# B and C of chunks 1 to 5 turned by VectorE's 32x32 transposes instead of TensorE's

## The chip, the cores and the metric

The kernel runs on one core of one Trainium2 chip. The metric is the device time of one execution in microseconds (us), lower is better; the time of before is the median of 8 runs. A profile is one further execution, recorded instruction by instruction.

Engines are named as the profile names them: PE is TensorE's matmul, PEld its weight load, DVE is VectorE, ACT is ScalarE, POOL is GpSimd, and SP is SyncE, which issues all DMAs of this kernel.

## The reference

Two blocks stand one behind the other. The first is a state-space scan over chunks (batch 4, 8 heads, 768 tokens, head size 32, state size 16):

```python
log_a = np.log(np.clip(a, 1e-06, 1.0))
for c in range(nc):
    cum = np.cumsum(la, axis=-1)
    L = np.exp(cum[:, :, :, None] - cum[:, :, None, :]) * causal
    M = np.einsum('bhin,bhjn->bhij', Cc, Bc) * L
    y_intra = np.einsum('bhij,bhjd->bhid', M, xc)
    y_inter = np.einsum('bhin,bhnd->bhid', Cc, state) * np.exp(cum)[:, :, :, None]
    y[:, :, sl] = y_intra + y_inter
    Bx = np.einsum('bhjn,bhjd->bhjnd', Bc, xc) * np.exp(cum[:, :, -1:] - cum)[:, :, :, None, None]
    state = np.exp(np.sum(la, axis=-1))[:, :, None, None] * state + np.sum(Bx, axis=2)
```

The second is a feed-forward layer over its output, 3072 tokens of 256 numbers, with 2048 hidden units:

```python
h = x @ w_in
relu6 = np.clip(h + 3.0, 0.0, 6.0)
out = (h * relu6 / 6.0) @ w_out
```

x, a, B and C come as float32. The two weights come as float64, so each word pair has to be decoded to float32 on the core.

## The kernel before

The 768 tokens are cut into 6 chunks of 128, and a chunk holds all 4 batches and 8 heads. The order of the work on every engine is written out by hand: each engine runs its instructions in program order, and SP issues the DMAs in program order too, so a DMA whose buffer isn't free holds back those behind it.

The program has a start and six passes. Pass k runs the feed-forward layer on chunk k, and in its gaps the scan of chunk c = k + 1; for chunk `ahead` = k + 2 it loads the data and makes the decays.

- *Start, to about 24 us.* Loads, logarithms, decays of chunk 0 and half of chunk 1, the scan of chunk 0.
- *Pass 0.* 16 calls of `mlp_in` (L445, h = w_in times y), into which the decoding of the weights is woven: 8 raw pieces of 1 MB (4 of w_in, 4 of w_out), 3 buffers, and `decode` (L154) in five steps on ACT and DVE each. `load_w` (L103) issues the next piece in the fourth step. Then 16 blocks of `first_out` (L533, the product with w_out), in four rounds i of four batches b; round i needs decoded piece 4 + i. Between the blocks stand the turn, the scores and the mixing of chunk 1, and sums of weights (`in_weight_sums`, L464, two halves of four sums; `weight_sums`, L556, four sums), which passes 1 to 5 need.
- *Passes 1 to 5.* The layer by sums of quarter blocks: 8 steps s of `early`, `lead`, `last` and `middle` (7 half products a step, L490), and 14 `out_units` (L599). In `lead` an odd and an even bank are begun; ACT copies one half of the odd bank to the even one, DVE the other half to `up` (L504). In `middle` DVE adds `up` to the banks (L516, L517); `last` then writes on the half of the even bank that L517 has read.

The scan of a chunk has these steps. *Turn* (L335): B and C lie with the token on the partition and (head, state) in columns; PE turns them with an identity, four 128x128 transposes a call into one bank `t_ps`, for two batches, two calls a chunk. ACT copies B turned to `bT` (L347); C turned is written twice, each time with the heads of the other parity zeroed, as `cT` (L359 on DVE, or L356 on ACT), so that two heads share one product; and C turned times the exponentials of the cumulative decay `eto` gives `csT` (L365). *Scores* (L369): bT times cT into four banks `cb`, then L384 multiplies them into the decay matrices `L`. *Mix* (L387): csT with the state, L with x, and the new state. *Keep* (L423) copies y out. *Sum_y* (L480) forms the sums of y that the next pass needs.

`load_bc` (L81) loads a chunk's C and B with two DMAs, by token, in runs of 64 bytes. `load_eto` (L250) spreads each row of cumulative decay over the 16 partitions of its head, with 8 DMAs. `load_decay` (L244) spreads such rows over all partitions; GpSimd masks them (`conceal`), and ACT takes the exponentials (`decay`, L312). `ends` and `carry` prepare the state's update on GpSimd.

The turn of chunk 1 stands in pass 0, after the first block of round 2. The turn of chunk c in passes 1 to 4 stands at steps 3 and 5 of the same pass that uses it.

## Time and profile before

| what | us |
|---|---|
| median of 8 runs (369.97 to 371.53) | 370.18 |
| the profiled execution | 370.77 |
| its span, first to last instruction | 369.1 |
| PE busy in it | 362.4 |
| DVE busy | 229.1 |
| ACT busy | 190.4 |
| POOL busy | 134.3 |

What lies around the span (370.77 - 369.1 = 1.7 us) is no instruction's. Busy times overlap between engines. PE's busy time counts matmuls from start to a modelled end, so consecutive ones overlap, and a wait can hide under the end of the one before; spacing of starts tells more. In the rows quoted below, "x8" is the number of instructions in a row, and "[0.29 <-DVE csT L365]" is idle time of the engine before it and what ended it. Rows with SPq are DMA issues: the time is that of SP's issuing, not of the transfer. DMAs moved 29.21 MB in 86689 packets, 75456 of them under 512 bytes.

### The profile page before, as it was taken

To read this page: it belongs to the slowest core of one execution; us is meant where nothing else is said; L and a number is where in the kernel's file an instruction comes from. 1 tells how busy PE (TensorE), PEld (TensorE's weight loads), DVE (VectorE), ACT (ScalarE), POOL (GpSimd) and SP (SyncE) were. 2 spreads that over 40 slices of the span, in tenths; PEclk is the share of its full clock that TensorE was granted. 3 is DMA by queue.
4 is the path that set the end of the run, shared out by engine and by line. 5 is a ranking of instruction groups with operands and counts; after the bars stand their busy time and mean duration, and the time that the engine had idled before them with its cause. 6 is when DMAs were issued, how large, how long until landed. Compare 5 with 4: busy or idle time off the path is not lost.

```text
span 369.1 us, 7275 instructions
## 1 busy us (share of the span) xinstructions
PE 362.4 (98%) x2893; PEld 307.9 (83%) x2893; DVE 229.1 (62%) x448; ACT 190.4 (52%) x414; POOL 134.3 (36%) x134
## 2 busy tenths in 40 slices
PE   7999999999999999999999999999999999999996
PEld 3664468778888899888899888999888989888996
DVE  7679999894897542787452688343588442488111
ACT  5858778776673830674650575560466100366100
POOL 1200020531499412099512088600058800057800
PEclk9999999999999999999999999999999999999999
DMA  8957999702790036910027830000000000000000
GB/s 164 207 220 172 165 372 118 254 5 76 239 114 3 2 97 204 120 10 2 2 55 247 93 36 0 2 17 15 28 3 1 2 2 30 28 1 2 2 28 28
DMA packets 86689, 29.21 MB, mean 79 GB/s; under 512 B 75456, under 2 KB 81248, under 8 KB 86656
## 3 DMA queue, kind: packets, MB, share of 16 engines
q1 hardware_dynamic: 86656, 28.76, 37.7%
q8 instruction: 22, 0.36, 0.4%
q14 instruction: 11, 0.09, 0.1%
HBM read 25.53 MB, written 3.23 MB: 78 GB/s over the span
## 4 chain that ended last, share of the span: by engine, by line
PE 84%; DVE 9%; ACT 4%; issue 1%; DMA 1%; ACTq 0%
PE even L490 19%; PE ob L599 17%; PE oa L599 17%; PE odd L490 14%; PE cb L376 4%; PE y L409 3%; PE o L540 3%; DVE gT L529 2%; DVE wm L178 2%; PE y L400 2%; ACT we L175 2%; ACT L L312 1%; PE t_ps L343 1%; PE d L289 1%; PE d L292 1%
## 5 line engine op out<-in xcount | busy, mean ns | idle before, releaser
L585 POOL TENSOR_TENSOR s<-gT 128x512 f32<-128x512 f32 x20 | 26.4, 1321 | 104.4 <-DVE gT L529 104.4
L490 PE MATMUL even<-ts,w_sum 128*128 128x256 f32 x160 | 48.2, 383 | 0.0
L524 ACT ACTIVATE gT<-odd,half 128x512 f32<-128x512 f32 x40 | 27.5, 687 | 35.4 <-DVE odd L517 35.4
L503 ACT COPY even<-odd 128x512 f32<-128x512 f32 x40 | 23.0, 575 | 43.0 <-PE odd L490 42.0
L312 ACT ACTIVATE L<-L,cum_n 128x128 f32<-128x128 f32 x144 | 43.2, 391 | 2.1 <-POOL L L303 2.1
L490 PE MATMUL odd<-yT,w_in 128*128 128x256 f32 x160 | 41.1, 379 | 0.0
L384 DVE TENSOR_TENSOR L<-L,cb 128x512 f32<-128x512 f32 (+1 forms) x56 | 30.4, 606 | 17.2 <-PE cb L376 17.2
L599 PE MATMUL oa<-w_out,gT 128*128 128x128 f32 x320 | 39.3, 278 | 0.0
L599 PEld LDWEIGHTS oa<-w_out,gT 128*128 128x128 f32 x320 | 38.1, 192 | 1.4 <-issue 0.2
L303 POOL TENSOR_SCALAR_AFFINE_SELECT L<-L 128x1024 f32<-128x1024 f32 x18 | 20.0, 1124 | 49.3 <-DMA L<-cum_d 49.1
L599 PE MATMUL ob<-w_out,s 128*128 128x128 f32 x320 | 37.8, 276 | 0.0
L599 PEld LDWEIGHTS ob<-w_out,s 128*128 128x128 f32 x320 | 36.5, 192 | 1.3 <-issue 1.3
L490 PEld LDWEIGHTS even<-ts,w_sum 128*128 128x128 f32 x160 | 29.9, 190 | 5.3 <-ACT up L510 1.5
L529 DVE SCALAR_TENSOR_TENSOR gT<-gT,odd 128x512 f32<-128x512 f32 x40 | 27.5, 687 | 9.9 <-ACT gT L524 9.7
L490 PEld LDWEIGHTS odd<-yT,w_in 128*128 128x128 f32 x160 | 30.1, 190 | 3.9
L524 ACT ACTIVATE gT<-even,half 128x512 f32<-128x512 f32 x40 | 27.8, 695 | 4.4 <-PE even L490 4.4
L529 DVE SCALAR_TENSOR_TENSOR gT<-gT,even 128x512 f32<-128x512 f32 x40 | 27.2, 680 | 4.4 <-ACT gT L524 4.4
L599 PE MATMUL ob<-t,gT 128*128 128x128 f32 x240 | 29.7, 277 | 0.0
L599 PEld LDWEIGHTS ob<-t,gT 128*128 128x128 f32 x240 | 28.0, 192 | 1.3 <-issue 1.3
L540 PE MATMUL o<-w_out,gT 128*128 128x256 f32 x128 | 28.9, 381 | 0.0
L504 DVE COPY up<-odd 128x256 f32<-128x256 f32 x40 | 16.9, 423 | 18.2 <-ACT even L503 14.4
L448 PE MATMUL h<-yT,w_in 128*128 128x512 f32 x64 | 27.7, 594 | 0.0
(110 smaller groups left out, 633.7 us busy)
## 6 DMA issues: line engine op xcount, KB each, us to landing
L<-cum_d SPq DMA_DIRECT2D x18, 512.0 KB, 6.5
raw<-in_moe_w_in_dram SPq DMA_DIRECT2D x4, 1024.0 KB, 8.2
raw<-in_moe_w_out_dram SPq DMA_DIRECT2D x4, 1024.0 KB, 8.8
xt<-in_x_dram SPq DMA_DIRECT2D x6, 512.0 KB, 8.6
out_dram<-res SPq DMA_DIRECT2D x20, 128.0 KB, 1.7
bc<-in_C_dram SPq DMA_DIRECT2D x6, 256.0 KB, 5.2
bc<-in_B_dram SPq DMA_DIRECT2D x6, 256.0 KB, 7.6
eto<-cum_d SPq DMA_DIRECT2D x40, 32.0 KB, 5.3
```

The costliest lines, as they stand in the source:

```text
L303: nc.gpsimd.affine_select(out=L, in_=L, pattern=[[0, NH], [1, P]], compare_op=ALU.is_ge, fill=-1e5, base=0, channel_multiplier=-1)
L312: nc.scalar.activation(L[:, h], L[:, h], AF.Exp, bias=cum_n[:, c, g:g + 1])
L384: nc.vector.tensor_tensor(out=L[:, :, hs], in0=L[:, :, hs], in1=cbs[q][:, in_pair], op=ALU.mult)
L448: nc.tensor.matmul(out=h.rearrange("p r i -> p (r i)"), lhsT=w_in[:, j, f * P:(f + 1) * P], rhs=yTs[k][:, j].rearrange("p b i -> p (b i)") ...
L490: nc.tensor.matmul(out=bank[:, r], lhsT=lhsT, rhs=rhs, start=start, stop=True, skip_group_check=True)
L503: nc.scalar.copy(out=even, in_=odd[:, 1:2].to_broadcast([P, 2, 2 * P]))
L504: nc.vector.tensor_copy(out=up[:, 1], in_=odd[:, 0])
L524: nc.scalar.activation(gTs[k][:, f], h.rearrange("p r i -> p (r i)"), AF.Relu, bias=half, scale=1.0 / 6.0)
L529: nc.vector.scalar_tensor_tensor(out=g, in0=g, scalar=1.0, in1=h.rearrange("p r i -> p (r i)"), op0=ALU.min, op1=ALU.mult)
L540: nc.tensor.matmul(out=o[:, b % 2], lhsT=gTs[0][:, f, b * P:(b + 1) * P], rhs=w_out[:, f], start=(f == 0 and b % 2 == 0), stop=True, skip_ ...
L585: nc.gpsimd.tensor_tensor(out=o, in0=p_, in1=q_, op=op)
L599: nc.tensor.matmul(out=bank[:, slot], lhsT=lhs[:, j], rhs=rhs[:, j], start=(clear and j == 0), stop=True, skip_group_check=True)
```

## The change

Chunk 0 is turned as before, by PE. For chunks 1 to 5:

- The turn is DVE's. Its transpose turns each 32x32 block by itself. C and B are loaded a second time in a layout for that (`by_pair`): partition group q holds heads 2q and 2q + 1, so a block has 32 tokens by (2 heads, 16 states); 8 DMAs each for C and B, with runs of 256 bytes. B by token is loaded as well, for the state's update; C by token no longer. All `by_pair` tiles share two buffers.
- C turned is written to `csT`, B turned to `bT`, for all four batches at once. Two multiplications by the parity give `cT` from `csT`, and then `csT` is multiplied by `eto` in place. The three tiles have one buffer each, not two.
- `load_eto` goes by batch: 4 DMAs over all 128 partitions in place of 8 over 16.
- In pass 0 the loads of chunk 1 are spread: B and the pieces of C at f = 0, the pieces of B at f = 4 (the fifth raw piece of the weights is issued at f = 3), x at f = 5. The loads of chunk 2 move behind the rows of chunk 2's decays.
- Chunk 1 is turned right behind the last weight piece, at (i, b) = (0, 0), and the exponential of its `eto` stands ahead of the decays. GpSimd's `carry` and `ends` stay at (2, 0), without the turn.
- The sums of weights move: the first half of `in_weight_sums` from (1, 0) to (2, 2), the second from (2, 1) to (3, 1), the first two of `weight_sums` from (2, 2) to (3, 2), the third from (3, 0) to the store half of pass 1, beside the fourth.
- Chunk 2 is turned in three parts at steps 1, 3 and 5 of pass 1. Chunk `ahead` is turned in unit 9 of the store half of passes 1 to 3, so chunks 3 to 5 are turned one pass earlier than before.

```diff
@@ -76,21 +76,42 @@
     a_sb = pre[:G, 0:2].rearrange("g t i -> g (t i)")[:, :S]
     nc.sync.dma_start(out=a_sb, in_=a.rearrange("b h s -> (b h) s"))
 
-    loaded = {}
+    Bs, bcs, xts = {}, {}, {}
 
     def load_bc(c):
+
+
         sl = slice(c * P, (c + 1) * P)
-        bc = loads.tile([P, 2, NB * NH, N], FP32, name="bc")
-        for j, src in enumerate((C, B)):
-            nc.sync.dma_start(
-                out=bc[:, j], in_=src[:, :, sl, :].rearrange("b h s n -> s (b h) n"))
-        loaded[c] = bc
+
+        def by_token(src, **where):
+            t = loads.tile([P, NB * NH, N], FP32, **where)
+            nc.sync.dma_start(out=t, in_=src[:, :, sl, :].rearrange("b h s n -> s (b h) n"))
+            return t
+
+        def by_pair(src):
+            t = loads.tile([P, 2, NB, 4, N], FP32, name="by_pair", tag="bc")
+            for b in range(NB):
+                for h in range(2):
+                    nc.sync.dma_start(
+                        out=t[:, h, b].rearrange("s a n -> s (a n)"),
+                        in_=src[b, h:NH:2, sl, :].rearrange("h (s a) n -> h s (a n)", a=4))
+            return t
+
+        if c == 0:
+            bcs[c] = [by_token(C, name="C", tag="bc")]
+            Bs[c] = by_token(B, name="B")
+            bcs[c].append(Bs[c])
+        else:
+            Bs[c] = by_token(B, name="B")
+            bcs[c] = []
+            for src in (C, B):
+                bcs[c].append(by_pair(src))
+                yield
 
     def load_x(c):
         sl = slice(c * P, (c + 1) * P)
-        xt = loads.tile([P, NB * NH, D], FP32, name="xt")
-        nc.sync.dma_start(out=xt, in_=x[:, :, sl, :].rearrange("b h s d -> s (b h) d"))
-        loaded[c] = loaded[c], xt
+        xts[c] = loads.tile([P, NB * NH, D], FP32, name="xt")
+        nc.sync.dma_start(out=xts[c], in_=x[:, :, sl, :].rearrange("b h s d -> s (b h) d"))
 
     w_in = const.tile([P, NK, DF], FP32, name="w_in")
     w_sum = const.tile([P, NF // 2, P], FP32, name="w_sum")
...
@@ -249,10 +271,10 @@
 
     def load_eto(c):
         eto = att.tile([P, NB, P], FP32, name="eto")
-        for h in range(NH):
+        for b in range(NB):
             nc.sync.dma_start(
-                out=eto[h * N:(h + 1) * N],
-                in_=cum_d[c, h:NB * NH:NH].unsqueeze(0).to_broadcast([N, NB, P]))
+                out=eto[:, b],
+                in_=cum_d[c, b * NH:(b + 1) * NH].unsqueeze(1).to_broadcast([NH, N, P]))
         etos[c] = eto
 
     cum_n = const.tile([P, NC, G], FP32, name="cum_n")
...
@@ -332,43 +354,56 @@
                 out=tmps[c], in0=states[c - 1],
                 in1=etos[c][:, :, P - 1:P].to_broadcast([P, NB, 2 * D]), op=ALU.mult)
 
-    def turn(c, p):
-
-
-        bc, xt = loaded[c]
-        pool, tag = (ps, "f") if c < 2 else (ps_o, "o")
-        t_ps = pool.tile([P, 4, P], FP32, name="t_ps", tag=tag)
+    def turned(c):
+        if c not in bTs:
+            bTs[c] = [att.tile([P, 2, 2, P], FP32, name="bT", bufs=1),
+                      att.tile([P, 2, 2, 2, P], FP32, name="cT", bufs=1),
+                      att.tile([P, 2, 2, P], FP32, name="csT", bufs=1) if c else None]
+        return bTs[c]
+
+    def turn(p):
+
+
+        c = 0
+        bT, cT, csT = turned(c)
+        t_ps = ps.tile([P, 4, P], FP32, name="t_ps", tag="f")
         for k in range(4):
             j, b = k // 2, 2 * p + k % 2
             nc.tensor.transpose(
                 out=t_ps[:, k],
-                in_=bc[:, j, b * NH:(b + 1) * NH].rearrange("s h n -> s (h n)"), identity=ident)
-        bT = att.tile([P, 2, P], FP32, name="bT")
-        nc.scalar.copy(out=bT, in_=t_ps[:, 2:4])
-        if c == 1 and p == 0:
-            from_start(c)
-            carry(c)
-            for b in range(NB):
-                ends(c, b)
-        cT = att.tile([P, 2, 2, P], FP32, name="cT")
-        if c == 1 or (c, p) == (0, 1):
+                in_=bcs[c][j][:, b * NH:(b + 1) * NH].rearrange("s h n -> s (h n)"),
+                identity=ident)
+        nc.scalar.copy(out=bT[:, p], in_=t_ps[:, 2:4])
+        if p:
             for t in range(2):
                 nc.scalar.activation(
-                    cT[:, :, t], t_ps[:, 0:2], AF.Copy, scale=parity[:, t:t + 1])
+                    cT[:, p, :, t], t_ps[:, 0:2], AF.Copy, scale=parity[:, t:t + 1])
         else:
             nc.vector.tensor_tensor(
-                out=cT, in0=t_ps[:, 0:2].unsqueeze(2).to_broadcast([P, 2, 2, P]),
+                out=cT[:, p], in0=t_ps[:, 0:2].unsqueeze(2).to_broadcast([P, 2, 2, P]),
                 in1=parity.unsqueeze(1).unsqueeze(3).to_broadcast([P, 2, 2, P]), op=ALU.mult)
-        csT = None
-        if c:
-            csT = att.tile([P, 2, P], FP32, name="csT")
-            nc.vector.tensor_tensor(
-                out=csT, in0=t_ps[:, 0:2], in1=etos[c][:, 2 * p:2 * p + 2], op=ALU.mult)
-        bTs[c, p] = bT, cT, csT
+
+    def turn_by_pairs(c):
+
+
+        bT, cT, csT = turned(c)
+        for t, out_ in zip(bcs[c], (csT, bT)):
+            nc.vector.transpose(
+                out=out_.rearrange("r p b (s a) -> r (p b) a s", a=4),
+                in_=t.rearrange("s t b a n -> s (b a) t n"))
+            yield
+        for t in range(2):
+            nc.vector.tensor_scalar(
+                out=cT[:, :, :, t].rearrange("r p b i -> r (p b) i"),
+                in0=csT.rearrange("r p b i -> r (p b) i"), scalar1=parity[:, t:t + 1],
+                scalar2=None, op0=ALU.mult)
+        nc.vector.tensor_tensor(
+            out=csT, in0=csT, in1=etos[c].rearrange("r (p b) i -> r p b i", p=2), op=ALU.mult)
+        yield
 
     def scores(c, bs):
 
-        bT, cT, csT = bTs[c, bs[0] // 2]
+        bT, cT = (t[:, bs[0] // 2] for t in bTs[c][:2])
         cbs = [ps.tile([P, 2, 2, P], FP32, name="cb", tag="f") for q in range(NQ)]
         for b in bs:
             for q in range(NQ):
@@ -387,14 +422,14 @@
     def mix(c, bs):
 
 
-        xt = loaded[c][1]
+        xt = xts[c]
         if bs[0] % 2 == 0:
             y_pss[c] = [ps_y.tile([P, 4, P], FP32, name=f"y{u}", tag=f"y{u}") for u in range(NK)]
         y_ps = y_pss[c]
         if c:
 
             for b in bs:
-                csT = bTs[c, b // 2][2]
+                csT = bTs[c][2][:, b // 2]
                 for q in range(NQ):
                     rows, d0 = slice(32 * q, 32 * q + 32), 2 * D * (q % 2)
                     nc.tensor.matmul(
...
@@ -738,7 +774,6 @@
     keep(0, 1)
     weights(1, 3)
     load_eto(1)
-    load(1)
 
 
     weave = {}
@@ -754,11 +789,16 @@
                 mlp_in(k, f)
                 for i in weave.get(f, []):
                     weights(i, 1)
+                if f == 0:
+                    bc_loads = load_bc(c)
+                if f in (0, 4):
+                    next(bc_loads)
+                if f == 5:
+                    load_x(c)
                 if f in (6, 8):
                     b = f // 2 - 1
                     load_decay(c, b)
                     conceal(c, b)
-            load(ahead)
             weights(NP + 1, 1)
             weights(NP + 3, 1)
             weights(NP + 2, 3)
@@ -771,36 +811,40 @@
                         weights(NP + 2, 1)
                         weights(NP + 3, 3)
                         rows(ahead)
+                        load(ahead)
+                        from_start(c)
                         decay(c, 2)
                         decay(c, 3)
-                    elif (i, b) == (1, 0):
-                        next(sums_in)
+                        for _ in turn_by_pairs(c):
+                            pass
                     elif (i, b) == (2, 0):
-                        turn(c, 0)
-                        turn(c, 1)
+                        carry(c)
+                        for b_ in range(NB):
+                            ends(c, b_)
                         for b_ in range(NB):
                             conceal(ahead, b_)
                     elif (i, b) == (2, 1):
                         scores(c, (0, 1))
-                        next(sums_in)
                     elif (i, b) == (2, 2):
                         decay_ends(ahead, 0)
-                        next(sums)
-                        next(sums)
+                        next(sums_in)
                     elif (i, b) == (2, 3):
                         results(c, 0)
                         scores(c, (2, 3))
                         decay_ends(ahead, 1)
                     elif (i, b) == (3, 0):
-                        next(sums)
                         decay_ends(ahead, 2)
                     elif (i, b) == (3, 1):
                         results(c, 1)
                         sum_y(c)
+                        next(sums_in)
                         decay_ends(ahead, 3)
                         from_start(ahead)
                     elif (i, b) == (3, 2):
                         lead(c, 0)
+                        next(sums)
+                        next(sums)
+            turns = turn_by_pairs(ahead)
             rows(ahead + 1)
             continue
         for s in range(NJ):
@@ -820,11 +864,11 @@
                 times_ramp(k, 2 * s - 2, evens[k, s - 1])
             ramp(k, 2 * s + 1, odds[k, s])
             times_ramp(k, 2 * s + 1, odds[k, s])
+            if k == 1 and s in (1, 3, 5):
+                next(turns)
             if s in (1, 3) and ahead < NC:
                 conceal(ahead, s - 1)
                 conceal(ahead, s)
-            if s in (3, 5) and c < NC:
-                turn(c, s // 4)
             if s in (2, 4, 6):
                 g_sums(k, s - 2)
         for i, _ in enumerate(out_units(k)):
@@ -835,6 +879,7 @@
                 times_ramp(k, 2 * s, evens[k, s])
                 g_sums(k, s - 1)
                 if k == 1:
+                    next(sums)
                     next(sums)
             if c < NC:
                 if i in (2, 4):
@@ -850,6 +895,9 @@
                     sum_y(c)
                     if ahead + 1 < NC:
                         rows(ahead + 1)
+                if i == 9 and ahead < NC:
+                    for _ in turn_by_pairs(ahead):
+                        pass
                 if i == 12:
                     lead(c, 0)
```

More of the change, by code (lines that the diff above doesn't have):

```diff
@@ L116 @@
     load_w(0)
-    load_bc(0)
+    for _ in load_bc(0):
+        pass
     load_x(0)
@@ L323, in ends @@
             nc.gpsimd.tensor_tensor(
-                out=bss[c][:, hs], in0=loaded[c][0][:, 1, hs],
+                out=bss[c][:, hs], in0=Bs[c][:, hs],
                 in1=decays_of(c, b)[:, :, P - 1:P].to_broadcast([P, NH, N]), op=ALU.mult)
@@ L667, in load @@
     def load(c):
-        load_bc(c)
+        for _ in load_bc(c):
+            pass
         load_x(c)
@@ L719 @@
     diff_fill(1, 0)
-    turn(0, 0)
-    turn(0, 1)
+    turn(0)
+    turn(1)
     diff_fill(1, 1)
@@ L773 @@
                         rows(ahead)
+                        load(ahead)
+                        from_start(c)
                         decay(c, 2)
                         decay(c, 3)
-                    elif (i, b) == (1, 0):
-                        next(sums_in)
+                        for _ in turn_by_pairs(c):
+                            pass
                     elif (i, b) == (2, 0):
-                        turn(c, 0)
-                        turn(c, 1)
+                        carry(c)
+                        for b_ in range(NB):
+                            ends(c, b_)
                         for b_ in range(NB):
@@ L852 @@
                         rows(ahead + 1)
+                if i == 9 and ahead < NC:
+                    for _ in turn_by_pairs(ahead):
+                        pass
                 if i == 12:
```

## The prediction

> **What bounds the kernel now.** I read the shares and the slices of the profile's page first, then the busy time in windows cut at the pass borders.
>
> ```profile
> PE 362.4 (98%) x2893; PEld 307.9 (83%) x2893; DVE 229.1 (62%) x448; ACT 190.4 (52%) x414; POOL 134.3 (36%) x134
> ...
> PE   7999999999999999999999999999999999999996
> ```
>
> ```profile
> 23.90:86.20 62.30, 62.01 (x353) 40.76 (x354) 59.12 (x87) 49.02 (x94) 11.28 (x14) 1.00 0.78 166
> 86.20:143.70 57.50, 57.50 (x498) 51.32 (x497) 33.68 (x69) 31.37 (x79) 30.73 (x29) 1.00 0.49 109
> 143.70:200.70 57.00, 57.00 (x506) 51.68 (x505) 32.40 (x68) 29.12 (x72) 26.52 (x25) 1.00 0.38 72
> ```
>
> The columns after the length are PE, PEld, DVE, ACT and POOL, then PE's granted clock (1.00), DMA share and GB/s. A busy PE may hide waits, so I also took the spacing of matmul starts in the timeline: 0.216 us for a 128x256 matmul, kept almost everywhere after 24 us. PE is the bound in every pass; pass 0 (23.9 to 86.2 us) has VectorE at 95% beside it. What PE no longer issues is therefore saved, unless another engine makes it wait. Now the turning of B and C, by tile:
>
> ```profile
> L343 PE MATMUL t_ps<-ident,bc x48: 272/273/273, 13.7 to 278.8; 128*128 128x128 f32 x48
> L347 ACT COPY bT<-t_ps x12: 350/366/373, 14.4 to 279.9; 128x256 f32<-128x256 f32 x12
> L365 DVE TENSOR_TENSOR csT<-t_ps,eto x10: 414/416/425, 69.4 to 281.2; 128x256 f32<-128x256 f32 x10
> L359 DVE TENSOR_TENSOR cT<-t_ps,parity x9: 683/683/692, 14.8 to 280.6; 128x512 f32<-128x512 f32 x9
> ```
>
> A transpose lasts 273 ns but is pipelined; what it costs PE is its spacing. That, and what chunk 1's turn costs in pass 0, stand in PE's timeline:
>
> ```profile
> 67.00 1.04 PE L343 MATMUL t_ps<-ident,bc 128*128 128x128 f32 x8
> 67.87 1.89 PE L540 MATMUL o<-w_out,gT 128*128 128x256 f32 x8
> 69.70 0.91 PE L376 MATMUL cb<-cT,bT 32*128 32x256 f32 x6
> 70.90 1.12 PE L376 MATMUL cb<-cT,bT 32*128 32x256 f32 x10 [0.29 <-DVE csT L365]
> 71.95 3.72 PE L540 MATMUL o<-w_out,gT 128*128 128x256 f32 x16
> ```
>
> Eight transposes hold PE from 67.00 to 67.87, 0.87 us. The 16 score matmuls then take from 69.70 to 71.95, 2.25 us; the same 16 in pass 1 take 1.08 us in the chain (119.44 to 120.52). So 1.17 us are waits: on cT, and on the csT product that releases the bank of t_ps.
>
> **The change, part by part.**
>
> *PE.* Chunks 1 to 5 lose 8 transposes each: 0.87 us in each of passes 0 to 4, 4.35 us in all, on the path. ScalarE loses 10 bT copies of 366 ns and 4 masked copies; it bounds nothing here.
>
> *VectorE's price.* No 32x32 transpose stands in the trace. Of the rows of 128x512 f32, L384's mean is 682 ns and L529's 680 to 687; consecutive ones start 0.61 to 0.73 us apart. Lower end: half of L171's 686 ns for 1024 words, 0.34 us. Upper end: 1.46 us, a 128x512 sum at 75.09 us beside a busy GpSimd. I take 0.69 us, the nearest rows. A masked copy SBUF to SBUF: between 0.34 and 0.69, I take 0.42. A chunk costs 2x0.69+2x0.42+0.69 = 2.9 us instead of 2x0.68+2x0.42 = 2.2, so little changes in VectorE's sum; the place matters.
>
> The Trainium skill (VectorE: DVE Perf Modes, "The three transpose paths" and "Rules for kernel authors") advises TensorE for 128x128 turns into PSUM and gives VectorE 311 ns for 128x128 bf16. An estimate of four times that for 512 columns is 1.24 us a transpose; the sum below would then end near 367.3 us. The rule compares single operations; it does not say which engine bounds.
>
> *Pass 0.* Chunk 1's turn now stands behind the last w_out product, which ends at 66.77 us, where four weight sums stood (66.68 to 69.42). Two transposes and two masked copies at starts 0.65 and 0.38 us apart end at 68.9 us. PE, freed of 0.87 us, asks for the scores at 68.83. I allow 0.35 us of wait, 0.2 of it for the last raw piece (below). The wait for t_ps's bank is gone, as there is no t_ps. csT's product (0.69 us) runs beside the scores; its eto is ready, since its exponential is moved ahead of the 16 decays. Gain: 0.87+1.17-0.35 = 1.7 us. A transpose at 0.34 us makes it 2.0; at 1.46 us, 0.15.
>
> *SP's queue.* In the trace an issue waits once 8 DMAs are in flight:
>
> ```profile
> 26.99 0.37 SPq L113 DMA_DIRECT2D raw<-in_moe_w_out_dram  x1
> 27.46 5.45 SPq L253 DMA_DIRECT2D eto<-cum_d  x8
> 33.14 0.39 SPq L85 DMA_DIRECT2D bc<-in_C_dram  x1
> ```
>
> After raw and seven eto the eighth stands until raw lands at 32.6. Chunk 1 now issues 4 eto, B, 8 C pieces, raw, 8 B pieces, x. Issues of 0.45 us and landings in order (about 3.1 us for a raw piece, 2.8 for B by token, 3.4 for x, an estimated 0.17 for a 32 KB piece as for a 32 KB eto) give: second w_out piece down at about 42.5 us (before: needed at 47.7), third at 53 (needed 54.9), fourth at 57.2 against 56.8. The fourth delays ScalarE's ws copy (56.90) by 0.3 us and the chain after it by 0.2, counted above. Bounds of that delay: none, since the copy after it is bound by VectorE at 58.22, to 3 us. Loads for chunk 2 move behind chunk 2's decay rows; they stand at the buffer that chunk 1's transpose frees (67.5 us), end near 78 and are wanted at 97. The output store queued behind them is due after 81.
>
> The skill (DMA: Bandwidth & Descriptors, the table's minimum transfer for line rate) wants 512 B and over, and the pieces are 256 B. The runs they replace for C are 64 B, so by the rule too C gets no worse, and B's second copy is extra; 1.3 MB over five chunks.
>
> *Start of pass 1.* The second four weight sums (2.75 us by 66.68 to 69.42) now follow sum_y, and the w_out sums t3 and t2 (1.21 us each) follow the first up copy.
>
> ```profile
> 86.27 0.88 DVE L487 TENSOR_TENSOR ts<-yT,ts 128x256 f32<-128x256 f32 x2
> 88.48 0.42 DVE L504 COPY up<-odd 128x256 f32<-128x256 f32 x1 [1.33 <-ACT even L503]
> 91.92 0.42 DVE L504 COPY up<-odd 128x256 f32<-128x256 f32 x1 [3.01 <-DMA out_dram<-ob]
> 92.26 0.42 DVE L516 TENSOR_TENSOR odd<-odd,up 128x256 f32<-128x256 f32 x1
> 92.78 0.43 DVE L517 TENSOR_TENSOR odd<-even,up 128x256 f32<-128x256 f32 x1
> ```
>
> On the clock of before: sum_y to 87.15, sums to 89.95, up to 90.4, t3 and t2 to 92.8, up, then L517 ends at 94.1 instead of 93.21. PE's "last" half product overwrites what L517 reads and starts at 93.27 now, so it is 0.9 us later. If the sums run as slowly as beside GpSimd (3.9 us at 74.11), 2 us later; if ScalarE leaves VectorE nothing to wait for, 0. I take 0.9: GpSimd's row shows little there.
>
> *Inside pass 1* VectorE needs 2.8 us a step (92.26, 95.06, 97.87), PE 3.03 (14 matmuls). A transpose in steps 1 and 3 fits in the slack; the last block (2x0.38+0.69) in step 5 exceeds it by some 0.45 us where before lost 0.3. Pass 1: -0.87+0.9+0.15 = +0.2 us.
>
> *Passes 2 to 4.* The turn moves to the store half, in VectorE's idle stretch:
>
> ```profile
> 136.69 0.87 DVE L487 TENSOR_TENSOR ts<-yT,ts 128x256 f32<-128x256 f32 x2
> 140.17 0.42 DVE L624 TENSOR_TENSOR res<-oa,x 128x256 f32<-128x256 f32 x1 [2.61 <-PE oa L599]
> ```
>
> 2.61 us of cover for some 2.7; the next idle stretch (3.15 us) takes an overrun, so it costs nothing up to about 2.5 us a transpose. The steps also lose two VectorE blocks, with a PE gap of 0.12 us (168.5 us). Each pass gains 0.87+0.12; three make 3.0. Passes 5 and the start to 23.9 us keep their orders: nothing.
>
> **Sum:** -1.7+0.2-3.0 = -4.5 us. The profiled execution took 370.77 us (span 369.1 and 1.7 around it); that becomes 366.3. The median, 370.18, lies 0.6 below it: **365.7 us**.
>
> **The rivals.**
>
> 1. *Half of it eaten on VectorE.* Transposes at 1.46 us cost 1.5 more in pass 0 and about 1.1 in pass 1: 368.3 us; sums at 3.9 us in pass 1's start alone: 366.8. For it: VectorE at 95% in pass 0. Against: L529's 40 rows hold 680 ns beside GpSimd.
> 2. *Raw pieces late.* Sixteen small issues ahead of the third and fourth piece. The trace has ACT waiting 0.84 us for the fourth already. 3 us more go through decode to the scores: 365.7+2.8 = 368.5 us. Against: the queue holds fewer packets (2048 of 256 B for 4096 of 64 B).
> 3. *The other side: transposes so slow that VectorE bounds.* Place: between 66.77 us and the scores, twice, and steps 1 and 3 of pass 1. Each microsecond on a transpose costs up to 4 us there, so above 0.69+4.5/4 = 1.8 us a transpose the gain is gone; at 2.5 us, 373 us. For: outputs are written every fourth word, and no such row exists. Against: L171 reads every second word at full pace.
> 4. *PE's turns were free.* Then 370.2. Against: the gap-free starts.
>
> **How the numbers follow.** The sum 62 in 100 (364.4 to 367.0: transposes between 0.34 and 1.0 us, pass 1's start at 0 to 2); rival 1 15, rival 2 9, rival 3 9, rival 4 5. The range 364.3 to 369.0 holds the first three for the most part. Below 369.4 (faster by over 0.2%, about what can be told here): 62+15+8 = 85; within: 5; above 370.9: 10.
>
> **What would show it.** Right: no t_ps row after 16 us; transposes near 0.69 us; scores of chunk 1 about 69 us, in 1.1 us; passes 2 to 4 near 56.0 us instead of 57.0; a PE gap near 92 us behind L517's counterpart. Wrong: a transpose over 1 us, ACT waiting over 1.5 us on the fourth piece, or passes 2 to 4 unchanged.

## The result, and the profile after

The changed kernel takes 375.47 us, the median of 11 runs (373.95 to 377.37), against 370.4 us for the kernel before on the same chips: 1.0131 times the time, interval 1.0113 to 1.015. It is slower, and the prediction of 365.7 us (364.3 to 369.0) was wrong, in sign too.

The page's shares and slices of the changed kernel:

```profile
PE 358.8 (96%) x2853; PEld 303.8 (81%) x2853; DVE 245.8 (66%) x455; ACT 185.7 (50%) x400; POOL 137.0 (37%) x134
...
PE   7899999699996999999999999999999999999996
...
PEclk9999999989998999999999999999999999999999
```

PE's busy time fell by 3.6 us. But there are two 6s in its slices, and an 8 in the granted clock in the slice behind the first and in the slice of the second: at about 70 and 116 us PE waits, and then runs at a lower clock. The busy time in windows cut at the pass borders (columns as before):

```profile
23.26:89.04 65.78, 61.90 (x344) 40.50 (x345) 57.37 (x83) 46.87 (x87) 12.49 (x14) 0.97 0.68 165
89.04:151.67 62.63, 58.67 (x490) 50.93 (x488) 49.12 (x82) 30.68 (x77) 32.17 (x29) 0.97 0.42 106
151.67:207.69 56.02, 56.02 (x498) 50.91 (x497) 35.59 (x69) 28.58 (x70) 26.51 (x25) 1.00 0.34 76
```

Read by pass, from the first matmul on h and the first `lead` of each pass (before: 23.89, 86.18, 143.54 us and so on):

| stretch | before | after | change | forecast |
|---|---|---|---|---|
| start | 23.89 | 23.26 | -0.6 | 0 |
| pass 0 | 62.29 | 65.78 | +3.5 | -1.7 |
| pass 1 | 57.36 | 62.63 | +5.3 | +0.2 |
| passes 2 to 4 | 170.63 | 167.62 | -3.0 | -3.0 |
| pass 5 | 54.89 | 54.84 | 0 | 0 |

The start has the same order in both kernels, and in the profiles of all kernels of this study it lies between 22.9 and 24.7 us; its -0.6 is that spread. The whole loss is in passes 0 and 1.

**Pass 0.** PE's timeline around chunk 1's scores:

```profile
66.14 3.72 PE L575 MATMUL o<-w_out,gT 128*128 128x256 f32 x16 [1.33 <-DVE w_out L213]
...
72.41 1.15 PE L411 MATMUL cb<-cT,bT 32*128 32x256 f32 x16 [2.55 <-DVE cT L396]
73.48 5.41 PE L575 MATMUL o<-w_out,gT 128*128 128x256 f32 x16
```

PE stands for decoded w_out (1.49 us by the spacing of starts, 1.33 idle), and for cT (2.71 by starts). The scores themselves then take 1.07 us without a stop, as forecast. The third line is the surprise: 16 matmuls in 5.41 us, where the first line has 16 in 3.72. VectorE in the same stretch:

```profile
68.28 1.32 DVE L213 SCALAR_TENSOR_TENSOR w_out<-wm,we 128x1024 f32<-128x1024 f32 x1
69.52 1.08 DVE L391 STREAM_TRANSPOSE csT<-by_pair 128x512 f32<-128x512 f32 x1
70.46 1.06 DVE L391 STREAM_TRANSPOSE bT<-by_pair 128x512 f32<-128x512 f32 x1
71.38 0.97 DVE L396 TENSOR_SCALAR cT<-csT,parity 128x512 f32<-128x512 f32 x2
72.46 1.39 DVE L400 TENSOR_TENSOR csT<-csT,eto 128x512 f32<-128x512 f32 x1
```

The last w_out product ends at 69.6 us; before it ended at 66.77. The turn behind it takes 2.8 us to cT, not the 2.1 of the forecast. Why the product is late stands in ScalarE's timeline, with two waits of 3.08 and 2.92 us for raw pieces of w_out where before had one of 0.84, and in SP's issues:

```profile
56.69 1.13 ACT L187 COPY ws<-raw 128x1024 uint16<-128x1024 uint16 x1 [3.08 <-DMA raw<-in_moe_w_out_dram]
...
60.73 1.13 ACT L187 COPY ws<-raw 128x1024 uint16<-128x1024 uint16 x1 [2.92 <-DMA raw<-in_moe_w_out_dram]
```

```profile
29.51 0.45 SPq L88 DMA_DIRECT2D B<-in_B_dram  x1
30.01 8.87 SPq L95 DMA_DIRECT2D by_pair<-in_C_dram  x8
38.99 0.40 SPq L134 DMA_DIRECT2D raw<-in_moe_w_out_dram  x1
39.49 6.32 SPq L95 DMA_DIRECT2D by_pair<-in_B_dram  x8
...
49.30 0.37 SPq L134 DMA_DIRECT2D raw<-in_moe_w_out_dram  x1
```

Eight small issues hold SP for 8.87 and 6.32 us. One lasts 0.54 us (the median of 40), and the first one behind B stood 4.78 us, though only six DMAs had gone out since 26.3 us (a raw piece, four `eto` and B). The third raw piece of w_out left at 49.30 us, before at 43.33.

**Pass 1.** VectorE and GpSimd at the last part of chunk 2's turn, and PE there:

```profile
113.86 1.27 POOL L620 TENSOR_TENSOR gT<-gT 128x512 f32<-128x512 f32 x1
114.09 2.73 DVE L396 TENSOR_SCALAR cT<-csT,parity 128x512 f32<-128x512 f32 x2
115.08 1.45 POOL L620 TENSOR_TENSOR s<-gT,s 128x512 f32<-128x512 f32 x1
116.85 0.69 DVE L400 TENSOR_TENSOR csT<-csT,eto 128x512 f32<-128x512 f32 x1
```

```profile
115.00 0.59 PE L525 MATMUL even<-ts,w_sum 128*128 128x256 f32 x2
118.81 1.22 PE L525 MATMUL even<-yT,w_sum 128*128 128x256 f32 x2 [3.21 <-DVE odd L552]
```

Two masked copies take 1.32 and 1.48 us beside GpSimd's sums. In unit 9 of pass 3, GpSimd idle, they take 0.42 and 0.47. In the same unit of pass 2 the first takes 0.42, and the second starts beside GpSimd's `conceal`:

```profile
203.84 1.09 POOL L325 TENSOR_SCALAR_AFFINE_SELECT L<-L 128x1024 f32<-128x1024 f32 x1 [3.20 <-DMA L<-cum_d]
203.89 1.32 DVE L396 TENSOR_SCALAR cT<-csT,parity 128x512 f32<-128x512 f32 x1
```

Each of these three slow copies ends 0.28 to 0.29 us after the GpSimd instruction that was running when it began: at 115.42, 116.82 and 205.21 us, behind ends at 115.13, 116.53 and 204.93. In unit 9 VectorE has idle time and PE doesn't wait for it, so the slow copy there costs nothing; at step 5 of pass 1 it does. In pass 1 PE waits 3.37 us by starts for VectorE's step behind them. Smaller waits are 0.91 us at the start of the pass and 0.13 each at steps 1 and 3. What follows both long waits is seen in short windows (PE's granted clock is the third number from the end):

```profile
73.90:77.30 3.40, 3.40 (x10) 2.69 (x9) 3.40 (x5) 1.88 (x7) 3.40 (x4) 0.50 0.24 53
77.30:80.00 2.70, 2.70 (x46) 2.07 (x48) 2.20 (x4) 0.00 (x0) 0.40 (x1) 1.00 0.26 59
...
118.30:121.60 3.30, 2.79 (x7) 2.25 (x8) 2.14 (x4) 1.64 (x3) 2.10 (x2) 0.50 0.00 0
```

For 3.41 us the clock is 0.50, and matmul starts are 0.427 us apart instead of 0.216. At most half of 3.41 us, 1.7 us, is lost each time (the second time PE is still idle for the first 0.54 us). With this upper value the passes add up. Pass 0: 1.49 + 2.71 + 1.7 - 0.87 (transposes) - 1.17 (old waits) = +3.9, measured +3.5. Pass 1: 0.91 + 0.26 + 3.37 + 1.7 - 0.87 = +5.4, measured +5.3. The executions of this kernel spread with the clock: 373.95 and 374.26 us at a mean granted clock of 1.0, 377.08 and 377.37 at 0.986; even the first two are 3.5 us above the kernel before. By this comparison the lower clock makes 1.2 to 1.5 us of the median's 5.1; the rest is waits, net of what is saved.

### The profile page after: what moved, and what is told of

Read it like the earlier page. It is cut to its first block, busy times and chain, and to the rows that moved or that the text cites. A ratio compares the mean times of both kernels' runs of the same rounds, so it can differ in the third digit from the quotient of the medians.

```text
span 374.1 us, 7253 instructions
## 1 busy us (share of the span) xinstructions
PE 358.8 (96%) x2853; PEld 303.8 (81%) x2853; DVE 245.8 (66%) x455; ACT 185.7 (50%) x400; POOL 137.0 (37%) x134
## 4 chain that ended last, share of the span: by engine, by line
PE 74%; SPq 7%; DVE 7%; DMA 6%; ACT 4%; issue 1%; DVEq 0%; ACTq 0%
PE ob L634 17%; PE oa L634 17%; PE even L525 16%; PE odd L525 12%; PE cb L411 4%; SPq L95 4%; PE y L444 3%; PE o L575 3%; DMA raw<-in_moe_w_out_dram 3%; DMA eto<-cum_d 2%; PE y L435 2%; DMA raw<-in_moe_w_in_dram 1%; SPq L269 1%; ACT L L320 1%; DVE cT L396 1%
## 5 line engine op out<-in xcount | busy, mean ns | idle before, releaser
L620 POOL TENSOR_TENSOR s<-gT 128x512 f32<-128x512 f32 x20 | 26.3, 1317 | 107.4 <-DVE gT L564 107.4
L575 PE MATMUL o<-w_out,gT 128*128 128x256 f32 x128 | 30.7, 398 | 1.3 <-DVE w_out L213 1.3
L575 PEld LDWEIGHTS o<-w_out,gT 128*128 128x128 f32 x128 | 25.2, 199 | 6.5 <-DVE w_out L213 1.7
L525 PE MATMUL even<-yT,w_sum 128*128 128x256 f32 x80 | 25.2, 397 | 4.0 <-DVE odd L552 4.0
```

Of the source, the lines that this page charges most:

```text
L525: nc.tensor.matmul(out=bank[:, r], lhsT=lhsT, rhs=rhs, start=start, stop=True, skip_group_check=True)
L575: nc.tensor.matmul(out=o[:, b % 2], lhsT=gTs[0][:, f, b * P:(b + 1) * P], rhs=w_out[:, f], start=(f == 0 and b % 2 == 0), stop=True, skip_ ...
L620: nc.gpsimd.tensor_tensor(out=o, in0=p_, in1=q_, op=op)
```

## The experiments

My theory: chunk 1's small loads delay the raw pieces (pass 0), and VectorE's masked copies beside GpSimd stop PE (pass 1). The rivals: slow transposes, the moved sums, or the turn by VectorE as such.

### The loads and the masked copies, each by itself

The loads of chunk 1 behind the raw pieces:

```diff
-                if f == 0:
+                if f == 12:
                     bc_loads = load_bc(c)
-                if f in (0, 4):
+                if f in (12, 13):
                     next(bc_loads)
```

> The pieces of C and B of chunk 1, and B by token, are issued at f = 12 and 13, behind the last raw piece (issued in the changed kernel at 50.33 us), not at f = 0 and 4. Theory (SP's order: 16 small issues of 0.58 us and one that stood 4.8 us hold back the third and fourth w_out piece): raw issues come back to about 43 and 48 us, ScalarE's waits for these pieces fall from 6.0 us to under 1.2, PE's wait for w_out (1.49 us) goes, its wait for chunk 1's scores falls from 2.71 to 1.0 to 1.5 us, the clock isn't halved in pass 0, and pass 0 goes from 38.2 to 33.5 to 35 us, the median from 375.5 to about 371.5. Rival (it is the bytes, not the order): waits for raw stay over 3 us, pass 0 over 37 us. Rival (the transposes are all of it): ScalarE's waits go, the score wait stays over 2.3 us and the clock still halves; about 373.5.

Measured: 374.76 us, 1.0102 times before (1.0017 to 1.0186). The raw pieces leave at 34.90, 41.91 and 49.62 us, ScalarE's waits for them are gone, and so is PE's wait for w_out. But the wait for cT stays. PE and VectorE in this run:

```profile
63.83 6.21 PE L575 MATMUL o<-w_out,gT 128*128 128x256 f32 x28
72.58 1.83 PE L411 MATMUL cb<-cT,bT 32*128 32x256 f32 x16 [2.54 <-DVE cT L396]
```

```profile
70.10 2.42 DVE L396 TENSOR_SCALAR cT<-csT,parity 128x512 f32<-128x512 f32 x2
```

The masked copies now take 1.20 and 1.31 us, because GpSimd's `conceal` starts earlier (69.93 us instead of 72.03) and so lies beside them. Half clock follows here too. Counted from the start of the first product with w_out, as the expectations count it, pass 0 is 36.66 us, 1.5 less than in the changed kernel (38.21) and not the 33.5 to 35 expected; the whole pass is 64.47 us instead of 65.78. The median isn't the 371.5 expected either. The queue's delay is real; once it is gone, the second cause takes its place in the same spot.

The masked copies on ScalarE:

```diff
-            nc.vector.tensor_scalar(
-                out=cT[:, :, :, t].rearrange("r p b i -> r (p b) i"),
-                in0=csT.rearrange("r p b i -> r (p b) i"), scalar1=parity[:, t:t + 1],
-                scalar2=None, op0=ALU.mult)
+            nc.scalar.activation(
+                cT[:, :, :, t].rearrange("r p b i -> r (p b) i"),
+                csT.rearrange("r p b i -> r (p b) i"), AF.Copy, scale=parity[:, t:t + 1])
```

> The two masked copies to cT are ScalarE's in chunks 1 to 5, all else as in the changed kernel. Theory (in pass 1 the two copies took 1.32 and 1.48 us on VectorE, held L552 and with it PE for 3.4 us, and that wait halved the clock for 3.4 us): the wait falls to 0.3 to 1.0 us, no half clock in pass 1, pass 1 goes from 62.6 to 57.5 to 59 us; pass 0 within 0.7 us of 38.2; passes 2 to 4 keep 56.0; median about 371. Rival (any work of VectorE in step 5 has this price, or ScalarE takes over as the one waited for): pass 1 stays over 61 us.

Measured: 373.05 us, 1.0065 (1.0035 to 1.0095). Pass 1 falls from 62.63 to 59.64 us; its 3.37 us wait becomes two of 0.84 and 0.56, and no half clock follows. Pass 0 keeps ScalarE's waits for raw pieces (5.3 us) and a wait for cT:

```profile
73.46 1.15 PE L410 MATMUL cb<-cT,bT 32*128 32x256 f32 x16 [2.93 <-ACT cT L396]
```

No half clock follows this one, though it is longer than the 2.55 us after which it came in the changed kernel. Pass 0 is 2.0 us shorter than in the changed kernel (63.79 us in all), where at most 0.7 was expected; pass 1 misses the 57.5 to 59 expected, and the median the 371.

Both edits together:

> The two earlier edits together: chunk 1's pieces of B and C behind the last raw piece, and the masked copies on ScalarE. Theory (late raw pieces and masked copies beside GpSimd are two causes in pass 0 that cover each other: either alone leaves a score wait of 2.7 to 3.1 us): the wait for w_out is gone, the score wait is 0.3 to 1.5 us, no half clock in the passes; pass 0 33 to 34.7 us, pass 1 about 59.6, median 368.5 to 370.5. Rival (the transposes' 1.1 us, or ScalarE's 16 decays ahead of the masks, keep the score wait over 2 us): pass 0 over 35.5 us, median over 371.

Measured: 369.78 us, 0.9991 (0.9962 to 1.0019): the time of before. Pass 0 from the first product with w_out is 33.20 us, 1.5 less than before (34.72), with 0.88 us of wait left for the scores. But that first product comes 0.6 us later in the pass here, behind the decoding of its w_out, so the whole pass is 61.36 us, 0.9 less than before (62.29). So the two causes together explain pass 0's loss. Pass 1 stays at 60.55 us (59.6 were expected), 3.2 above before, in waits of 0.66, 1.02, 0.85 and 0.53 us at full clock: masked copies taken off VectorE don't make chunk 2's turn fit.

GpSimd's sums of step 4 written at step 6 instead, to clear the place of the masked copies:

```diff
-            if s in (2, 4, 6):
-                g_sums(k, s - 2)
+            if s in ((2, 6) if k == 1 else (2, 4, 6)):
+                for j in ((2, 4) if k == 1 and s == 6 else (s - 2,)):
+                    g_sums(k, j)
```

> In pass 1 GpSimd's four sums of step 4 are done with those of step 6; nothing else moves. Theory (VectorE's masked copies from SBUF are slow because GpSimd runs beside them: 0.40 to 0.47 us where GpSimd is idle, 1.32 to 1.48 beside its sums): the two copies in step 5 take 0.4 to 0.5 us each, PE's wait falls from 3.4 to 1.1 to 1.7 us, the clock isn't halved in pass 1, pass 1 falls from 62.6 to about 59 us, median about 372. Rival (the copies are slow by their shape or their place behind the pair loads): they stay at 1.3 to 1.5 us, time within 0.5 us of 375.5.

Measured: 376.36 us, 1.0157. It tells nothing of the copies: nothing else of GpSimd's stands between the two places, so its own order stayed as it was, and the sums ran as soon as their inputs were there, at the same place. The masked copies still took 1.37 and 1.48 us. An edit in the program's order moves an engine's work only past other work of that engine.

### The price of the operations

Behind the last pass, on a tile that nothing reads, twice each: transposes with output in rows or at every fourth word, and input in one run or in two, then a 128x128 transpose, one of 16-bit words, a masked copy and a product. The main lines of the edit:

```diff
...
+    plain_in = src_.rearrange("s (m t n) -> s m t n", m=16, t=2)
+    apart_in = src_.rearrange("s (t b n) -> s b t n", t=2, n=16)
+    plain_out = dst_.rearrange("r (m s) -> r m s", m=16)
+    apart_out = dst_.rearrange("r (m s a) -> r m a s", m=4, a=4)
...
+        nc.vector.transpose(out=plain_out, in_=plain_in)
...
+        nc.vector.transpose(out=plain_out, in_=apart_in)
...
+        nc.vector.transpose(out=apart_out, in_=plain_in)
...
+        nc.vector.transpose(out=apart_out, in_=apart_in)
...
```

> Behind the last instruction of the changed kernel stand pairs of VectorE transposes of a filled tile that nothing reads, with GpSimd idle: 128x512 f32 with input and output in rows, with input in two runs of 16 apart, with the output at every fourth word, with both, then 128x128 f32, bf16 words, and one masked copy and one product of 128x512. Theory A (a transpose of 32-bit words costs about 1.1 us by itself): all four forms at 1.0 to 1.15 us. Theory B (the output at every fourth word costs it): 0.65 to 0.75 us in the first two, 1.1 in the others. Theory C (the input in two runs costs it): 0.65 to 0.75 us in the first and third. Masked copy 0.40 to 0.47, product 0.69.

VectorE's timeline there:

```profile
372.81 1.46 DVE L912 STREAM_TRANSPOSE form<-form 128x512 f32<-128x512 f32 x2
374.30 1.46 DVE L914 STREAM_TRANSPOSE form<-form 128x512 f32<-128x512 f32 x2
375.79 2.19 DVE L916 STREAM_TRANSPOSE form<-form 128x512 f32<-128x512 f32 x2
378.01 2.19 DVE L918 STREAM_TRANSPOSE form<-form 128x512 f32<-128x512 f32 x2
```

Each row is two instructions: 0.73 us each with output in rows, 1.10 with output at every fourth word, whatever the input. The price that I took, 0.69, is near that of the first form; the kernel uses the other. The masked copy takes 0.49 us here and the product 0.69.

The kernel's operations, three each, beside eleven sums on GpSimd and then with GpSimd idle:

```diff
...
+    for _ in range(11):
+        nc.gpsimd.tensor_tensor(out=beside[:, 0], in0=src_, in1=src_, op=ALU.add)
+    vector_ops()
+    nc.vector.memset(src_, 1.0)
+    vector_ops()
```

> Behind the last instruction of the changed kernel VectorE runs, on a filled tile that nothing reads afterwards, three masked copies, three products of two SBUF inputs, three transposes with output in rows and three with output at every fourth word (all 128x512 f32), first beside eleven sums of GpSimd (about 14 us), then with GpSimd idle. Theory (GpSimd's running work slows those of VectorE's operations that read SBUF by two streams: masked copies and products; single-stream ones, so the transposes, not): masked copy about 0.5 us alone and 1.2 to 1.5 beside, product 0.7 alone and over 1.0 beside, transposes 0.73 and 1.1 us in both. Rival (the slow copies in the kernel are its own affair, such as their output in four runs): masked copies 0.5 us in both.

The timeline of VectorE and GpSimd:

```profile
371.84 2.85 DVE L914 TENSOR_SCALAR form<-form,parity 128x512 f32<-128x512 f32 x3
371.94 13.55 POOL L924 TENSOR_TENSOR beside<-form 128x512 f32<-128x512 f32 x11 [17.71 <-DVE form L907]
374.72 4.30 DVE L917 TENSOR_TENSOR form<-form 128x512 f32<-128x512 f32 x3
...
381.29 3.35 DVE L921 STREAM_TRANSPOSE form<-form 128x512 f32<-128x512 f32 x3
386.19 1.53 DVE L914 TENSOR_SCALAR form<-form,parity 128x512 f32<-128x512 f32 x3
387.75 2.15 DVE L917 TENSOR_TENSOR form<-form 128x512 f32<-128x512 f32 x3
...
392.17 3.30 DVE L921 STREAM_TRANSPOSE form<-form 128x512 f32<-128x512 f32 x3
```

The first masked copy began 0.11 us ahead of GpSimd's first sum and took 0.49 us, as with GpSimd idle. The second, beside that sum, took 1.14 (1.2 to 1.5 were expected), and so did the third:

```profile
371.94 1.28 POOL L924 TENSOR_TENSOR beside<-form 128x512 f32<-128x512 f32 x1 [17.71 <-DVE form L907]
372.36 1.14 DVE L914 TENSOR_SCALAR form<-form,parity 128x512 f32<-128x512 f32 x1
```

A product takes 1.41 us beside GpSimd instead of 0.69; a transpose takes 1.12 instead of 1.10 by the rows, the same. So GpSimd's presence makes the two kinds dearer that the forecast had at 0.42 and 0.69, and only them.

How much dearer follows from when they end. The second masked copy ends at 373.50 us, 0.28 us after the sum at 373.22. Over the eight traces with masked copies on VectorE, 36 of them began while a GpSimd instruction was running, and all 36 ended 0.28 to 0.29 us after that instruction, whether it was a sum, a product or `conceal`; they lasted 0.63 to 1.48 us. Of the other 42, all but one took 0.40 to 0.49; that one, 1.39 us long, began 0.02 us ahead of a `conceal` and ended 0.28 us after it. The products go the same way: 26 of the 28 that began beside GpSimd ended 0.54 to 0.55 us after its instruction, and the other two took 0.69 us. So these kinds aren't slowed by a factor; they are held until GpSimd's running instruction has ended. The output in four separate runs, which the kernel's masked copies have and the copies here don't, adds nothing: both end 0.28 us behind.

The Trainium skill (SBUF — State Buffer, "Who interferes with whom") says that VectorE and GpSimd share a pair of ports, which an instruction holds to its end, and that a VectorE operation with two inputs in SBUF, or a copy-like one in a two-port mode, contends for it. These rows agree in which kinds suffer, and in the holding: a masked copy beside GpSimd ends a fixed 0.28 us after GpSimd's instruction, a product mostly 0.54 to 0.55.

### Which of the turned chunks pays

Chunks 0 to 2 turned by PE, with the loads and the sums of before, and only chunks 3 to 5 by VectorE in unit 9:

```diff
-        if c == 0:
+        if c <= 2:
             bcs[c] = [by_token(C, name="C", tag="bc")]
...
-            if k == 1 and s in (1, 3, 5):
-                next(turns)
+            if k == 1 and s in (3, 5):
+                turn(c, s // 4)
```

> Chunks 0 to 2 are turned by PE, with loads, sums and places of before; chunks 3 to 5 as in the changed kernel (VectorE, unit 9 of passes 1 to 3). Theory (the gain of passes 2 to 4 is real and whole, and all the loss lies in passes 0 and 1): passes 2 to 4 at 56.0, 56.0 and 55.6 us, pass 0 34.7, pass 1 57.4 (both as before); median 3.0 us under before, 367.2 (366.6 to 367.8). Rival (the gain needs something that passes 0 and 1 of the changed kernel do): under 1.5 us.

Measured: **367.70 us**, 0.9917 times before (0.9883 to 0.995), the best of all. Its passes 1 and 2 in windows:

```profile
85.50:143.00 57.50, 57.47 (x498) 51.23 (x497) 38.36 (x74) 31.43 (x79) 30.75 (x29) 1.00 0.47 115
143.00:199.00 56.00, 56.00 (x499) 50.90 (x498) 35.58 (x69) 28.57 (x70) 26.52 (x25) 1.00 0.34 76
```

Pass 0 (61.93 us) and pass 1 (57.43) stand as before, and passes 2 to 4 take 56.02, 56.02 and 55.57 us: the 3.0 us gain is whole.

The same, with the sums moved as in the change:

> As e7 (chunks 0 to 2 by PE, 3 to 5 by VectorE late), with the sums of weights moved as the change moves them and nothing else. Theory (the moved sums alone are what makes PE wait 0.9 us at the start of pass 1): that wait is there, 0.8 to 1.0 us, pass 1 58.0 to 58.6 instead of 57.4; pass 0 no longer than 34.7; median 368.3 to 369.0 against 367.7 of e7. Rival (the wait comes of pass 0's delays): none at that place, median as e7.

Measured: 368.1 us, 0.9955 (0.9937 to 0.9972). PE waits 0.91 us near the start of pass 1, and the pass takes 58.30 us in the profile, 0.87 more; the intervals of the two times meet, so the times alone don't tell these kernels apart.

```profile
92.78 0.70 PE L533 MATMUL even<-yT,w_sum 128*128 128x256 f32 x2 [0.74 <-DVE odd L560]
```

Chunks 0 and 1 by PE, with the sums of before, and chunk 2 by VectorE in pass 1:

> Chunks 0 and 1 are turned by PE, with the loads of chunk 1 and the sums of weights placed as before; chunks 2 to 5 as in the changed kernel. Theory: pass 0 is back at 34.7 us; of pass 1's 62.6 the wait of 0.9 us at its start goes (it was the moved sums'), the wait behind step 5's masked copies (3.4 us) and the half clock after it stay: 61.5 to 62; passes 2 to 4 keep 56.0; median about 371.5. Rival (pass 1 suffers from what pass 0 leaves behind): pass 1 within 0.7 us of 57.4, median 367.5.

Measured: 372.14 us, 1.0037 (1.0016 to 1.0058). Pass 1 is 62.03 us, 4.6 more than with chunk 2 on PE, by this wait and the half clock from 115.2 us on:

```profile
110.17 0.59 PE L533 MATMUL even<-ts,w_sum 128*128 128x256 f32 x2
113.97 0.70 PE L533 MATMUL even<-yT,w_sum 128*128 128x256 f32 x2 [3.21 <-DVE odd L560]
```

The same, with the masked copies on ScalarE:

> As e8 (chunk 1 turned by PE, sums as before, chunks 2 to 5 by VectorE), with the masked copies on ScalarE. Theory (of e8's pass 1 at 62.0 us, 3.4 us are the wait behind the masked copies and 1.7 the half clock that it sets off; two transposes in steps 1 and 3 cost little): pass 1 57.4 to 58.3 us, no half clock, median 4 us under e8, 367.8 to 368.6. Rival (the transposes of 1.1 us in steps 1 and 3 and the product beside GpSimd in step 5 hold PE as well): pass 1 over 59 us, median over 369.2.

Measured: 369.73 us, 0.9989 (0.9968 to 1.0009), pass 1 58.68 us, at full clock. The wait at step 5 is 0.84 us behind ScalarE's `up` copy, which now queues behind the masked copies, and 0.55 behind VectorE. The pass missed the 57.4 to 58.3 expected, and the median the 367.8 to 368.6. So even without the slow copies VectorE's turn in pass 1 costs 1.25 us more than PE's.

## Why the prediction was wrong

- *What bounds the kernel: PE, and what it no longer issues is saved.* Right where VectorE has idle time (passes 2 to 4), and the -3.0 us of that step came exactly, in the changed kernel and with chunks 3 to 5 alone. The turn's price there was wrong (5.0 to 5.1 us from the first transpose to the product's end in passes 1 and 2, not 2.9); the step held because VectorE's idle time there took the overrun, as the forecast allowed. In passes 0 and 1 the exception that the sentence itself makes, "unless another engine makes it wait", was the case.
- *VectorE's price.* "A masked copy SBUF to SBUF: between 0.34 and 0.69, I take 0.42" failed. Of the rows that I bounded it by, L171 ran with GpSimd idle, and L384 and L529 have one operand in a bank that PE writes, where the masked copy has both ends in SBUF; they take 0.68 us beside GpSimd and without it. The slow rows beside GpSimd that I had found, the 1.46 us sum and the four sums in 3.9 us, I used as bounds for the transposes, which GpSimd doesn't slow, and for the sums at the start of pass 1, not for the masked copies. The trace of before had another: the w_out product at 49.29 us, beside `conceal`, takes 2.00 us instead of 1.23. Measured: 0.40 to 0.47 alone, 1.3 to 1.48 beside GpSimd at step 5, and the product 0.69 and 1.39. The transposes' 0.69 was off as well: 1.06 to 1.17. That is some 0.6 us of the late scores in pass 0, at starts 0.94 us apart instead of 0.65.
- *Inside pass 1: "exceeds it by some 0.45 us".* The wait is 3.37 us there. The block is 1.32 + 1.48 + 0.69 = 3.5 us instead of the 1.45 that I had, behind a step with 0.2 us of slack. With the half clock this is the largest loss, 4.6 us by the pair of kernels with chunk 2 on PE and on VectorE.
- *SP's queue: "The fourth delays ScalarE's ws copy (56.90) by 0.3 us".* The mechanism was the right one, the size wrong. ScalarE waited 6.0 us in all for the last two pieces, instead of 0.84; its copies of them start at 56.69 and 60.73 us, where the forecast had them down at 53 and 57.2. My 0.45 us an issue is 0.58 with the gap, and I let the pieces go out at once behind B, where the first stood 4.78 us: the reading that an issue waits once 8 DMAs are in flight didn't cover it, as it came seventh, counted from the raw piece at 26.37 us. Rival 2 had this mechanism at 3 us and 368.5 us; its removal alone brought 1.3 us of pass 0, because the masked copies then slowed down.
- *Pass 0: -1.7 us.* Not reached: with both causes taken away the pass is 0.9 us shorter than before.
- *Start of pass 1: 0.9 us.* Right: 0.91 in the changed kernel, and 0.91 with the sums moved alone.
- *The rivals.* Rival 3 held the sign, by transposes over 1.8 us: they take 1.1, so it didn't happen. Rival 1 was nearest in kind, VectorE dearer beside GpSimd, but with the slowness put on the wrong instruction. Of the three signs of being wrong, two came: transposes over 1 us, and ScalarE waiting over 1.5 us for the fourth piece (2.92).
- *Missing: the clock.* No step of the forecast gave a wait more than its own length. Here two waits were followed by 3.41 us at half clock, at most 1.7 us each, in the profiled execution; by the executions without it, the clock is 1.2 to 1.5 of the median's 5.1 us.

## What to carry to other kernels

Price each VectorE instruction beside what GpSimd is doing at the place where it will stand, by its own kind: masked copies and products with both ends in SBUF were held until GpSimd's running instruction ended, transposes weren't. Small loads put ahead of large ones cost the queue here by their issues, so count issues and what each stands behind. Of a change with the same edit in several stages, keep the stages with idle time: here three chunks of five gave the whole gain, 0.9917 times the time.

## What the runs showed of the hardware

- *Half clock after a stop of PE.* The length of the stop alone doesn't decide. Half clock followed idle times of 2.55 and 3.21 us in the changed kernel and 1.88 us in the run with GpSimd's sums moved. It didn't follow 2.93 us with the masked copies on ScalarE, nor 3.27 us in pass 1 with the loads moved, nor the 2.55 us of pass 0 in the run that prices the transposes, whose passes have the changed kernel's program. The traces show what does: the granted clock changes only on a grid. In the changed kernel its stretches last 68.27, 3.41, 40.96, 3.41 and 252.59 us, whole multiples of 3.413 us, and so it is in all twelve traces (but for a last stretch that the trace's end cuts). Two stops, in windows cut at the grid:

```profile
70.48:73.89 3.41, 1.48 (x18) 1.10 (x19) 3.31 (x6) 1.59 (x6) 2.23 (x3) 1.00 0.12 28
```

```profile
68.97:72.38 3.41, 1.56 (x8) 1.02 (x6) 3.23 (x3) 3.41 (x13) 1.99 (x4) 1.00 0.06 8
72.38:75.79 3.41, 2.33 (x22) 1.85 (x23) 1.98 (x3) 3.00 (x9) 3.41 (x4) 1.00 0.22 50
```

The first row is of the changed kernel: 1.93 us of its 2.55 fall in one window of the grid (PE is busy for 1.48 of 3.41), and the next is at half clock. The other two are of the run with the masked copies on ScalarE: a border of the grid cuts 2.93 us into 1.86 and 1.08, and no half clock follows. From the first h product on, in all twelve traces, each of the eight windows at full clock in which PE was idle for 1.88 to 2.67 us is followed by half clock, and none with 1.86 us or less is. Where a stop falls on the grid differs between executions of one kernel, so the same stop is followed by half clock in some of them only. Twice half clock lasted 6.83 us, in the two runs that price operations, where PE was idle for over 1 us of the first half-clock window too. At the start, before the h products, half clock came after windows with 0.41 to 0.86 us of idle time, so idle time alone isn't all that counts there. The Trainium skill (TensorE: Matmul & The Clock Gate, "What's actually happening") has a free-running window of 3.4 us and a halved clock after an idle one. The grid of 3.41 us and the 0.50 agree with it; that 1.88 us of idle time in a window were enough is not what the page says.
- *VectorE beside GpSimd.* A masked copy that begins while a GpSimd instruction runs ends 0.28 to 0.29 us after it (36 of 36), a product 0.54 to 0.55 (26 of 28), so what they cost is the time that GpSimd's instruction still has to run.
- *A transpose with its output at every fourth word* takes 1.10 us instead of 0.73; an input in two runs costs nothing. The Trainium skill (Advanced Engine Details and Errata, "SBUF Cachelines") says that accesses that each go to another 16-byte line are slower. A step of four words of float32 is such a line, so it agrees.
- *A DMA issue of a `by_pair` piece*, 32 KB, holds SP for 0.54 us, against 0.42 for an `eto` issue of 32 KB in the kernel before and 0.37 for a raw piece of w_out, 1 MB: the bytes don't set it.
